# Attention with a spectral mix on one core: a new hand-written order for the last loop, two pairs summed half by VectorE and half by GpSimd, and one pair's x taken earlier

## The chip, the cores and the metric

The kernel runs on one core of a Trainium2 chip. The metric is the device time of one execution in microseconds (us), as the median over several executions. Engines are named as in the profile: PE (TensorE matmul), PEld (its weight loads), DVE (VectorE), ACT (ScalarE), POOL (GpSimd), SP (the engine that issues most of the transfers on and from the chip at the end).

## What is computed

Eight batches, 8 heads, 576 tokens, 64 values a head. First a causal attention with a bias from a running sum of `s`, then a mixing layer over the 512 joined values:

```
attn = softmax(scale * q k^T + min(bias, 0), causal) ; x = attn v      # (8, 576, 512)
X = rfft(x, axis=1);  Y[:, :64] = X[:, :64] * (w_r + i w_i)            # one 512x512 matrix for each of 64 modes
y = irfft(Y, n=576);  u = x + y
out = u + relu(u @ w_ch)
```

The two mode weights have 64 x 512 x 512 values each in float32; reading them is the largest transfer of the program.

## The kernel before

**Stages.** Attention runs over 32 steps `n` (a pair of heads and a batch each), and the products of the modes, which need the weights as they arrive, are spread over these steps. GpSimd issues all weight loads (line 234), SP the small transfers and the output. After the attention comes the last group of modes: `modes(NG - 1, c)` for the chunks c = 0 to 7 of 8 modes each. Each chunk gives `yb` (line 487), its transpose `yt` (672), and for the later chunks `v = y @ w_ch` (680). The results must be regrouped by batch into `yv`: the early chunks by `gather`, which is matmuls into PSUM and copies by ACT and DVE in turn (lines 699, 709, 711), the last two by `spread`, a transfer on SP (line 498). All this shares two PSUM buffers (`auxpool`).

**Pairs.** The output is made in 18 pairs of token tiles, 0 to 17; pairs 1 and 15 are made of the short last tiles of four batches. Each needs z = (x + y) @ w_ch and u = x + y. The product x @ w_ch needs no y, so for the pairs 2 to 17 (`kept`) it is computed early and stored in SBUF (`keep`, or `first_product` for pairs 3 to 8 within the attention). For the pairs 0 and 1 it is left in PSUM: `x_transposed` (transposes, line 635, and DVE casts, 639) and then `x_times_wch` (648). The function `work` takes the kept pairs between the chunks.

**Ways.** How a stored product meets the rest is a letter for each pair:
- "g": ACT copies z (which is y @ w_ch) from PSUM (`relu`, line 795), GpSimd adds the stored product (`gpsimd_sum`, 803), DVE does max and sum in one instruction (`finish`, 819).
- "v": DVE adds z and the stored product (`kept_sum`, 812), then 819.
- "s": ACT writes the stored product into PSUM ahead of the matmuls (`seed`, 894), they add to it, ACT does the Relu (797), DVE adds u (821).
- "e": the product is stored as two half-precision numbers (526, 527), which PE adds by matmuls with the identity (`digits`, 899), then as "s".

**The last loop.** Its order is one string of steps, each a letter and a pair, with a or b for the half: X (x into the bank of u, 774), U (y into it, 744), Z (y @ w_ch, 744), S, E, K, R, G for the helpers above, and F, which sums and starts the output transfer. Each engine takes its instructions in the order of that string. Z has four PSUM banks, by parity of the pair and half, so a Z waits until the last pair of its parity has been read there. U has two double banks by parity, so X of a pair waits for F of the pair two before. The pairs in `x_pool` get their x from GpSimd (line 807) and not from X. Ahead of the loop, `first_u` and `first_z` start the pairs 0 and 1 between the products of the last chunk (the `meanwhile` of `modes`).

Of the kernel before, what the change touches and what calls it, by code (L numbers as in the profile page):

```python
# [18 lines left out]
def kernel(  # L19
# [20 lines left out]
    NG = DM // P  # L40
# [6 lines left out]
    NCK = NM // MC  # L47
# [155 lines left out]
    def ring_of(k):  # L203
        if k < NE:
            return None
        return int(k < LW2 and (k - NE) % (WA + WB) >= WA)
# [38 lines left out]
    for n in range(N):  # L245
# [3 lines left out]
        while nt < min(w, len(wq)):  # L249
            i = ring_of(nt)  # L250
# [245 lines left out]
    def spread(c, which, rows):  # L496

        nc.sync.dma_start(out=yv[16 * c : 16 * c + 16, :, which, :], in_=rows)
# [8 lines left out]
    kept = list(range(NPRE, len(pairs)))  # L507


    ways = dict(zip(kept, "gvgesggsgsgsgsgs"))  # L510

    first_pairs = [i for i in kept[1:] if pairs[i][0][1] < NF and pairs[i][0][0] <= 4][:6]
    z1s, xts1 = {}, {}
# [42 lines left out]
    with tc.tile_pool(name="sc_psum", bufs=2, space=PSUM) as scpool, \  # L556
# [7 lines left out]
        for n in range(N):  # L564
# [11 lines left out]
            i = first_pairs[n - N + len(first_pairs)] if n >= N - len(first_pairs) else None  # L576
# [46 lines left out]
    def parts(b, T):  # L623

        if T < NF:
            return [(slice(0, P), b, ident16h)]
        return [(slice(NL * i, NL * i + NL), b + i, ident16h[:NL, :NL]) for i in range(2)]

    def x_transposed(i):
        xts[i] = xt_sb[len(xts) % 2]  # L630
        for x, (b, T) in enumerate(pairs[i]):
            ps = upool.tile([P, DT, P], FP32, name="xt_ps", tag="u")
            for rows, bb, ident in parts(b, T):
                for dt in range(DT):
                    nc.tensor.matmul(
                        ps[:, dt, rows], x_all[: rows.stop - rows.start, dt, bb, T, :],
                        ident, start=True, stop=True, skip_group_check=True,
                    )
            nc.vector.tensor_copy(out=xts[i][:, x], in_=ps)  # L639

    def start_z(i, x):
        zs[i, x] = zpool.tile([P, DM], FP32, name="z_ps", tag=f"z{i % 2}{x}")

    def x_times_wch(i, last):
        for x in range(2):
            start_z(i, x)
            for dt in range(DT):
                nc.tensor.matmul(  # L648
                    zs[i, x], xts[i][:, x, dt, :], wch_sb[:, dt, :],
                    start=(dt == 0), stop=(last and dt == DT - 1), skip_group_check=True,  # L650
                )
# [25 lines left out]
    def y_times_wch(c, yt):  # L677
        vp = auxpool.tile([P, DM], FP32, name="v_ps", tag="aux")
        for dt in range(DT):
            nc.tensor.matmul(  # L680
                vp, yt[:, dt, :], wch_sb[:, dt, :], start=(dt == 0), stop=(dt == DT - 1)
            )
        vb = spool.tile([P, DM], FP16, name="v_sb", tag="v")
        nc.vector.tensor_copy(out=vb, in_=vp)
        spread(c, 1, vb)
        return vb

    def gather(c0, c1, turns, kinds):

        n = 2 * MC * (c1 - c0)  # L690
        rows = slice(2 * MC * c0, 2 * MC * c1)
        ng = P // n
        for b0 in range(0, B, ng):
            for which in kinds:
                ps = auxpool.tile([P, DM], FP32, name="g_ps", tag="aux")
                for dt in range(DT):
                    for g in range(ng):
                        op = yt_first[:, dt, : c1 - c0].rearrange("p c (x b) -> p (c x) b", b=B)
                        nc.tensor.matmul(  # L699
                            ps[n * g : n * g + n, :] if which else ps[n * g : n * g + n, bass.ts(dt, P)],  # L700
                            op[:, :, b0 + g],
                            wch_sb[:, dt, :] if which else ident16h,
                            start=(dt == 0 or not which), stop=(dt == DT - 1 or not which),
                            tile_position=(0, n * g), skip_group_check=True,
                        )
                for g in range(ng):
                    dst, src = yv[rows, b0 + g, which, :], ps[n * g : n * g + n, :]
                    if g % 2:
                        nc.vector.tensor_copy(out=dst, in_=src)
                    else:  # L710
                        nc.scalar.copy(out=dst, in_=src)
            if b0 // ng in turns:
                work()
# [4 lines left out]
    def work():  # L718

        if not order_z and not ahead:  # L720
            return
        if order_z:
            i = order_z.pop(0)
            x_transposed(i)
            ahead.append(i)
        if len(ahead) == 2 or not order_z:
            i = ahead.pop(0)
            keep(i)
# [3 lines left out]
    TAKE = (3, 2, 4, 0, 0, 0)  # L732
    us, rs = {}, {}
    last = len(pairs) - 1
    x_pool = (17,)
    direct = (2,)
    GK = P - 2 * MC * NX

# [41 lines left out]
    def u_of(i):  # L780
        return [us[i][:, x, :] for x in range(2)]
# [8 lines left out]
    def relu(i, x):  # L790

        if i not in rs:
            rs[i] = result(i)
        if ways.get(i) == "g":
            nc.scalar.copy(out=rs[i][:, x], in_=zs[i, x])
        else:
            nc.scalar.activation(out=rs[i][:, x], in_=zs[i, x], func=ACTF.Relu)

    def gpsimd_sum(i, x):

        r = rs[i][:, x]
        if ways.get(i) == "g":
            nc.gpsimd.tensor_tensor(out=r, in0=r, in1=z1s[i][:, x], op=ALU.add)
        else:
            b, T = pairs[i][x]
            r = r.rearrange("p (g d) -> p g d", d=P)
            nc.gpsimd.tensor_tensor(out=r, in0=r, in1=x_all[:, :, b, T, :], op=ALU.add)
# [6 lines left out]
    def finish(i, x=None):  # L814
        xx = slice(0, 2) if x is None else slice(x, x + 1)
        b, T = pairs[i][0]
        o, u = rs[i][:, xx, :], us[i][:, xx, :]
        if ways.get(i) in ("v", "g"):
            nc.vector.scalar_tensor_tensor(out=o, in0=o, scalar=0.0, in1=u, op0=ALU.max, op1=ALU.add)
        else:  # L820
            nc.vector.tensor_tensor(out=o, in0=u, in1=o, op=ALU.add)
        if T == NF:
            j = b // 2
            dst = out.rearrange("(j h) t e -> j (h t) e", h=2)[j : j + 2, NF * P : NF * P + P, :]
            nc.sync.dma_start(out=dst.rearrange("x p e -> p x e"), in_=o)
        else:
            dst = out[b, bass.ds(first_token(b, T + (x or 0)), P * (2 if x is None else 1)), :]
            nc.sync.dma_start(out=dst.rearrange("(x p) e -> p x e", p=P), in_=o)
# [4 lines left out]
    for c in range(NCK - 2):  # L833
        yb = modes(NG - 1, c)
        for x in range(TAKE[c] - 1):
            work()
        if c == NCK - 3:
            x_transposed(0)
        yt = y_transposed(yb, c)
        if TAKE[c]:  # L840
            work()
        if c >= NY:
            if c == NCK - 3:
                x_times_wch(0, False)
            y_times_wch(c, yt)
            if c == NCK - 3:
                gather(NY, NCK - 2, (), (0,))
        elif c == NY - 1:
            gather(0, NY, (1, 3), (1, 0))
    assert not order_z and not ahead  # L850
    c = NCK - 2
    yb6 = modes(NG - 1, c)
    x_transposed(1)
    yt = y_transposed(yb6)
    x_times_wch(1, False)
    vb6 = y_times_wch(c, yt)


    def first_u():
        add_x(0)  # L860
        add_y(u_of(0), 0, 0, slice(0, GK))
        add_last(u_of(0), 0, yb6, c=0)

    def first_z(i):
        add_y(z_of(i), i, 1, slice(0, GK))
        add_last(z_of(i), i, vb6, c=0)

    yb = modes(NG - 1, NCK - 1, {2: lambda: (first_u(), first_z(0)), 3: lambda: first_z(1)})

    yt = spool.tile([P, DT, P], FP16, name="yt_sb", tag="yt")  # L870
    for x in range(2):
# [49 lines left out]
        "F": finish,  # L921
    }
    for step in (
# [7 lines left out]
    ).split():  # L931
        i = int(step[1:].rstrip("ab"))
        if step[-1] in "ab":
            steps[step[0]](i, "ab".index(step[-1]))
        else:
            steps[step[0]](i)
# [30 lines left out]
```

The softmax here doesn't subtract the row's maximum and nothing guards it: scores larger than these inputs give would overflow.

## Time and profile before

| what | us |
|---|---|
| median of four executions | 444.44 |
| lowest, highest | 443.68, 445.47 |
| the profiled execution, its own time | 443.68 |
| its span, first to last instruction | 441.6 |
| busy over the span: PE, DVE, ACT, POOL | 343.8, 253.0, 226.4, 246.4 |
| output, 18 pairs of 512 KB: first and last transfer issued | 412.65, 438.0 |
| mean of one: line 803 POOL, 819 DVE, 821 DVE (a whole pair) | 1.28, 1.22, 1.22 |
| mean of one: line 795 ACT, 797 ACT, 894 ACT | 0.62, 0.63, 0.63 |

Times are counted from the start of the span. A group of instructions is shown with its busy time, the mean of one in ns, and the idle time of its engine just ahead of it with what ended that. Matmuls overlap, so their mean is longer than the step from one to the next. "Landing" is the time from the issue of a transfer to its end.

### The profile page before, as it was taken

What the parts mean: (1) busy time and instruction counts of PE and PEld (TensorE: products, weight loads), DVE (VectorE), ACT (ScalarE), POOL (GpSimd) and SP (SyncE); (2) the same over time, 40 slices, a digit from 0 to 9 for tenths busy, and PEclk for the clock granted to TensorE, in tenths of its full rate; (3) what the DMA queues carried; (4) which work ended last, traced back from release to release, by engine and by line L of the source; (5) the groups of instructions that cost most, each with busy time, mean ns of one, the idle gap of its engine ahead of it and who ended that gap; (6) DMA issues with size and microseconds to landing.
All of it is one profiled execution on the core that took longest, in us unless ns stands there. A gap on an engine that the chain in (4) does not pass through costs nothing.

```text
span 441.6 us, 10830 instructions
## 1 busy us (share of the span) xinstructions
PE 343.8 (78%) x4411; PEld 207.2 (47%) x4411; DVE 253.0 (57%) x574; ACT 226.4 (51%) x421; POOL 246.4 (56%) x385
## 2 busy tenths in 40 slices
PE   1688988998776996793946927988996887779994
PEld 1465665555554653462534504555553435434441
DVE  7766775675645664462633605667656443452696
ACT  1576785465644643472543514565661524420794
POOL 7766565565565656455655546555544444440495
PEclk9998998998969798898895968999999989988998
DMA  9999999999999999999999999999999999998498
GB/s 178 202 207 205 204 207 205 207 201 205 209 200 208 204 208 204 208 207 208 204 206 206 208 207 192 210 205 208 204 209 211 209 209 209 210 216 167 149 388 343
DMA packets 72768, 93.25 MB, mean 211 GB/s; under 512 B 29760, under 2 KB 31296, under 8 KB 72720
## 3 DMA queue, kind: packets, MB, share of 16 engines
q0 software_dynamic: 63408, 81.29, 105.0%
q1 hardware_dynamic: 9312, 11.29, 7.6%
q8 instruction: 34, 0.56, 0.5%
q14 instruction: 14, 0.11, 0.1%
HBM read 163.51 MB, written 9.44 MB: 392 GB/s over the span
## 4 chain that ended last, share of the span: by engine, by line
DMA 53%; PE 25%; DVE 11%; issue 4%; POOL 3%; ACT 3%; POOLq 0%; SPq 0%; DVEq 0%; ACTq 0%
DMA w_sb<-in_moe_w_i_dram 27%; DMA w_sb<-in_moe_w_r_dram 17%; DMA qk<-in_k_dram 4%; PE z_ps L648 4%; PE yp L463 4%; DMA qk<-in_q_dram 4%; PE sc_ps L382 3%; DVE qt L344 2%; PE av_ps L418 2%; PE sc_ps L376 2%; PE tr_ps L340 2%; POOL w_sb L234 2%; PE g_ps L699 1%; DVE kt L344 1%; DVE xs L453 1%
## 5 line engine op out<-in xcount | busy, mean ns | idle before, releaser
L390 ACT ACTIVATE p_sb<-sc_ps,cumt_sb 128x576 f16<-128x576 f32 (+1 forms) x256 | 141.8, 636 | 34.2 <-PE sc_ps L382 33.8
L234 POOL DMA_DIRECT2D w_sb<-in_moe_w_r_dram x120 | 71.2, 595 | 61.2 <-DMA w_sb<-in_moe_w_i_dram 16.7
L234 POOL DMA_DIRECT2D w_sb<-in_moe_w_i_dram x120 | 70.9, 593 | 51.4 <-DMA w_sb<-in_moe_w_i_dram 18.6
L382 PE MATMUL sc_ps<-qt,kt 128*128 128x512 bf16 (+2 forms) x384 | 78.1, 316 | 3.9 <-ACT kt L344 3.3
L344 DVE COPY qt<-tr_ps 64x576 bf16<-64x576 bf16 x64 | 47.8, 747 | 56.8 <-PE tr_ps L340 56.8
L234 POOL DMA_DIRECT2D v<-in_v_dram x72 | 52.1, 724 | 38.3 <-DMA w_sb<-in_moe_w_r_dram 10.2
L340 PE MATMUL tr_ps<-ident,qk 64*64 64x64 bf16 x1152 | 35.5, 206 | 39.7 <-DMA qk<-in_k_dram 17.6
L463 PE MATMUL yp<-w_sb,xs 128*32 128x512 bf16 (+1 forms) x480 | 43.9, 418 | 22.0 <-DMA w_sb<-in_moe_w_i_dram 14.8
L361 ACT ACTIVATE p<-sc_ps,cumt 128x64 f16<-128x64 f32 x32 | 10.1, 314 | 89.9 <-PE sc_ps L357 89.9
L376 PE MATMUL sc_ps<-negm,ident 128*128 128x256 bf16 x256 | 54.2, 297 | 0.0
L382 PEld LDWEIGHTS <-kt 128*128 128x128 bf16 x384 | 39.2, 106 | 31.5 <-ACT kt L344 8.7
L340 PEld LDWEIGHTS <-qk 64*64 64x64 bf16 x1152 | 27.0, 119 | 55.7 <-DMA qk<-in_k_dram 18.5
L418 PE MATMUL av_ps<-v,p_sb 128*128 128x65 f16 x1024 | 43.5, 196 | 1.5 <-DVE x_all L428 0.6
L418 PEld LDWEIGHTS <-p_sb 128*128 128x128 f16 x1024 | 37.0, 99 | 8.8 <-DVE x_all L428 4.2
L453 DVE CAST xs<-ft_ps 64x128 bf16<-64x128 f32 x128 | 36.6, 286 | 3.3 <-PE ft_ps L443 1.7
L463 PEld LDWEIGHTS <-xs 128*32 128x32 bf16 (+1 forms) x512 | 19.2, 145 | 40.4 <-DMA w_sb<-in_moe_w_i_dram 15.2
L423 DVE TENSOR_REDUCE den<-av_ps 128x5 f32<-128x10 f32 x64 | 10.8, 169 | 41.4 <-PE av_ps L418 40.4
L428 DVE TENSOR_TENSOR x_all<-av_ps,rcp 128x320 f16<-128x320 f32 x64 | 31.5, 491 | 2.2
L344 ACT COPY kt<-tr_ps 64x576 bf16<-64x576 bf16 x32 | 22.9, 715 | 14.7 <-DVE qt L344 14.1
L648 PE MATMUL z_ps<-wch_sb,xs 128*128 128x512 f16 x96 | 25.6, 415 | 0.2 <-DVE xs L639 0.2
L443 PE MATMUL ft_ps<-Ff_sb,x_all 128*64 128x192 f16 (+1 forms) x320 | 24.6, 268 | 1.0 <-DVE x_all L428 1.0
L483 DVE TENSOR_TENSOR y_acc<-yp,y_acc 128x512 f32<-128x512 f32 x16 | 11.1, 692 | 24.3 <-PE yp L463 23.5
(113 smaller groups left out, 435.3 us busy)
## 6 DMA issues: line engine op xcount, KB each, us to landing
w_sb<-in_moe_w_r_dram POOLq DMA_DIRECT2D x120, 256.0 KB, 8.5
w_sb<-in_moe_w_i_dram POOLq DMA_DIRECT2D x117, 256.0 KB, 9.0
out_dram<-r_w SPq DMA_DIRECT2D x16, 512.0 KB, 2.8
v<-in_v_dram POOLq DMA_DIRECT2D x72, 64.0 KB, 7.5
qk<-in_q_dram POOLq DMA_DIRECT2D x15, 288.0 KB, 8.4
qk<-in_k_dram POOLq DMA_DIRECT2D x15, 288.0 KB, 9.2
x_all<-in_moe_w_i_dram POOLq DMA_DIRECT2D x6, 256.0 KB, 7.7
y_acc<-in_moe_w_r_dram POOLq DMA_DIRECT2D x4, 256.0 KB, 7.8
```

The source lines that it names most:

```text
L234: nc.gpsimd.dma_start(out=dst, in_=src)
L340: nc.tensor.transpose(ps[rows, r, :], src[rows, r, :], ident16[rows, rows])
L344: copy(out=to[:, :, :, half * RH : half * RH + RH], in_=ps[HP * i : HP * i + HP].rearrange("d r (h p) -> d h p r", h=2),)
L376: nc.tensor.matmul(ps[:, bass.ds(w * S, W)], ident16, negm[:, bass.ts(r, W)], start=True, stop=False, skip_group_check=True,)
L382: nc.tensor.matmul(ps[:, c0 : c0 + i1 - i0], keys[:, w, r, :], qh[:, i0:i1], start=False, stop=True, skip_group_check=True,)
L390: nc.scalar.activation(out=pt[:, poff[x] : poff[x] + S - w * W], in_=ps[:, w * S : (w + 1) * S - w * W], func=ACTF.Exp, bias=cumt_sb[:, x, ...
L418: nc.tensor.matmul(ps[:, I, r : r + NCH], lhsT, rhs, start=(i == 0), stop=(i == len(todo) - 1), skip_group_check=True,)
L428: nc.vector.tensor_tensor(out=x_all[:, g, b, :, D * h : D * h + D], in0=ps[:, :, 1 : NCH], in1=rcp.unsqueeze(2).to_broadcast([P, NT, D]), ...
L443: nc.tensor.matmul(ps[HP * q_ : HP * q_ + HP].rearrange("p h f -> p (h f)"), x_all[:nT, g, b, T, q_::2], Ff_sb[:nT, T, :], start=(T == 0), ...
L453: nc.vector.tensor_copy(out=xs[g % 2][HP * h : HP * h + HP, q_, :, h, :, b, :], in_=a)
L463: nc.tensor.matmul(ps[32 * cg : 32 * cg + 32, :], cols[k0:, q_, 1 - ri, :, c * MC // 2 + cg], wt[(g, c, ri, cg // 2)][k0:, 2 * (cg % 2) + ...
L648: nc.tensor.matmul(zs[i, x], xts[i][:, x, dt, :], wch_sb[:, dt, :], start=(dt == 0), stop=(last and dt == DT - 1), skip_group_check=True,)
```

## The change

Pair by pair, 2 to 17, the ways go from `gvgesggsgsgsgsgs` to `vsgmsgsgmsgsgsgs`. A new letter "m" is treated by `relu`, `gpsimd_sum` and `finish` as "g" is; in the string, half a of such a pair (5 and 10) is a K on DVE and half b an R and a G. No pair is "e" any more. (The letter "n" is accepted and not used.) Pair 17 gets its x from PE. The order string of the last loop is another one. Ahead of the loop, the transposes of pair 1 stand before `y_times_wch` of chunk 5 and its products behind the second gather, and both `first_z` come ahead of `first_u`.

```
-    ways = dict(zip(kept, "gvgesggsgsgsgsgs"))
+    ways = dict(zip(kept, "vsgmsgsgmsgsgsgs"))
...
-    x_pool = (17,)
+    x_pool = ()
...
-        if ways.get(i) == "g":
+        if ways.get(i) in ("g", "m", "n"):
...
-        if ways.get(i) in ("v", "g"):
+        if ways.get(i) in ("v", "g", "m", "n"):
...
             if c == NCK - 3:
                 x_times_wch(0, False)
+                x_transposed(1)
             y_times_wch(c, yt)
             if c == NCK - 3:
                 gather(NY, NCK - 2, (), (0,))
+                x_times_wch(1, False)
...
     yb6 = modes(NG - 1, c)
-    x_transposed(1)
     yt = y_transposed(yb6)
-    x_times_wch(1, False)
     vb6 = y_times_wch(c, yt)
...
-    yb = modes(NG - 1, NCK - 1, {2: lambda: (first_u(), first_z(0)), 3: lambda: first_z(1)})
+    yb = modes(NG - 1, NCK - 1, {2: lambda: (first_z(0), first_z(1)), 3: first_u})
...
-        "R0a X1 R0b F0a U1 R1a F0b Z2a R1b Z2b R2a F1 X2 R2b G2a U2 Z4a Z4b R4a Z3a Z3b G2b K3a X3 R4b U3 "
-        "S6a K3b E5a S6b G4a F2 Z5a E5b R5a Z5b Z6a R5b Z7a G4b F3 Z6b X4 R6a Z7b R6b U4 R7a Z8a F4 Z8b X5 "
-        "R7b G7a U5 S9a S9b X6 F5 G7b U6 R8a Z9a R8b Z9b F6 X7 R9a G8a U7 R9b Z10a F7 Z10b S11a X8 G8b "
-        "S11b U8 R10a Z11a X9 R10b G10a U9 F8 R11a Z12a Z12b R12a Z11b F9 G10b X10 R12b U10 S13a Z14a R11b "
-        "Z14b G12a F10 Z13a R14a X11 U11 S13b Z16a G12b R13a F11 X12 R14b U12 S15a Z13b G14a Z16b F12 X13 "
-        "R13b U13 R16a Z15a G14b S15b F13 X14 R15a U14 R16b Z15b G16a F14 X15 S17a R15b U15 G16b S17b Z17a "
-        "F15 X16 R17a U16 Z17b G17a F16 U17 R17b G17b F17a F17b "
+        "R0a X1 R0b F0a U1 R1a F0b Z2a R1b Z2b S3a K2a X2 S3b F1 U2 Z3a Z3b R3a Z4a K2b X3 R4a U3 F2 R3b "
+        "G4a Z5a S6a Z4b Z5b R4b K5a Z6a X4 R5b G4b F3 U4 S6b Z7a Z7b R6a Z6b G5b F4 R7a X5 U5 R6b Z9a R7b "
+        "G7a F5 X6 S8a Z9b U6 S8b Z8a G7b R9a F6 X7 U7 R8a Z8b R9b G9a Z10a F7 X8 R8b U8 S11a Z10b K10a "
+        "G9b X9 S11b U9 F8 R10b Z12a Z11a G10b R12a Z12b Z11b F9 R12b X10 U10 R11a G12a Z14a R11b F10 Z14b "
+        "X11 S13a U11 G12b S13b Z13a F11 X12 R14a U12 R13a G14a Z16a Z13b R14b F12 X13 R13b U13 G14b S15a "
+        "Z16b F13 X14 S15b U14 R16a Z15a F14 Z15b R16b G16a X15 R15a U15 R15b G16b S17a X16 F15 S17b U16 "
+        "Z17a Z17b R17a F16 X17 R17b U17 F17a F17b "
```

More of the change, by code (lines that the diff above doesn't have):

```diff
@@ L801, in gpsimd_sum @@
         r = rs[i][:, x]
-        if ways.get(i) == "g":
+        if ways.get(i) in ("g", "m", "n"):
             nc.gpsimd.tensor_tensor(out=r, in0=r, in1=z1s[i][:, x], op=ALU.add)
```

## The prediction, made before the changed kernel ran

> **What bounds the kernel now.** I read the page's 40 slices first, then windows of 4 us over the end, the groups of the last loop by shape, the chain of its last 10 us, the output transfers by issue time, and last the granted clock on a fixed grid.
>
> ```profile
> span 441.6 us, 10830 instructions
> ...
> 412.00:416.00 4.00, 4.00 (x24) 1.62 (x20) 3.11 (x5) 3.53 (x8) 1.94 (x2) 1.00 0.56 206
> ...
> 420.00:424.00 4.00, 3.93 (x19) 1.65 (x17) 3.89 (x4) 4.00 (x9) 4.00 (x4) 1.00 0.95 370
> ...
> 432.00:436.00 4.00, 3.80 (x20) 1.08 (x18) 3.70 (x4) 3.51 (x7) 3.73 (x4) 1.00 1.05 408
> 436.00:440.00 4.00, 0.00 (x0) 0.00 (x0) 1.62 (x3) 0.00 (x0) 1.29 (x2) 0.85 1.03 400
> ```
>
> The columns are window, PE, PEld, DVE, ACT, POOL, clock, DMA share, GB/s. Until 405 the weights fill the DMA engines. From 411.3 the last loop runs, and from 420 everything in it is full: PE, ACT, POOL, nearly DVE, and from 428 the output DMA too.
>
> ```profile
> L803 POOL TENSOR_TENSOR r_w<-r_w,z 128x512 f32<-128x512 f32 x12 | 14.9, 1277 | 0.8 <-ACT r_w L795 0.8
> L819 DVE SCALAR_TENSOR_TENSOR r_w<-r_w,u_ps 128x1024 f32<-128x1024 f32 x9 | 10.9, 1219 | 1.3 <-POOL r_w L803 1.2
> L797 ACT ACTIVATE r_w<-z_ps 128x512 f32<-128x512 f32 x16 | 9.5, 628 | 0.5 <-PE z_ps L744 0.3
> ...
> 434.35 0.60 ACT r_w L797
> 434.95 0.07 issue
> 435.02 1.15 POOL r_w L807
> 436.17 1.12 POOLq L962
> 437.30 0.02 issue
> 437.32 0.69 DVE r_w L821
> ```
>
> The idle columns are almost empty. The chain ends in pair 17: two GpSimd additions of x in series between the last Relus and the last sums. POOLq L962 is the second of them.
>
> ```profile
> L234 POOL DMA_DIRECT2D w_sb<-in_moe_w_i_dram x1: 590/590/590, 396.6 to 396.6; - x1
> DMA to landing us min/median/max: 10.5/10.5/10.5
> ...
> 407.15 0.19 PEld L463 LDWEIGHTS <-xs 128*32 128x32 bf16 x4 [0.42 <-DMA w_sb<-in_moe_w_i_dram]
> ```
>
> The last weights land at 396.6 + 10.5 = 407.1, and the products that need them start at 407.15. So what stands ahead of the loop is tied between PE and the weights.
>
> **The change, part by part.**
>
> *x of pair 1 moved.* Its transposes (16 matmuls, 0.96 in the chain) go ahead of y_times_wch of chunk 5, its 8 matmuls (2.98) behind the second gather. Before, both stood after chunk 6's modes. With them move two DVE casts (1.28 for both), now ahead of chunk 5's v_sb. Second v_sb and gather slip by about 0.65. PE idled 392.98 to 394.86 while yv was copied, and the 8 matmuls (1.83 at full clock, as the same group took at 380.7) fit there. Chunk 6's modes then start near 395.45 instead of 394.86, but their second half waits for weights until 396.35 either way. Behind it PE is freed of about 3.9. SP's order stays: the spread of chunk 6's v only goes out about 3 us sooner (near 400.4 instead of 403.53), with no output transfer to pass. POOL's weight issues keep their order, at a constant landing of 10 to 10.6. **Sum: 0**, because the weights still land at 407.1. Without that cover it would be up to 3.9 of gain. Swapping first_u and first_z reorders 1.40 against 0.98 ahead of the same last product: 0.
>
> *Ways.* By number of instructions in the loop, with the step from one start to the next read from runs of the same instruction:
> - POOL: 18 to 14. Four of about 1.25 go, two of them at the very end (2.27).
> - ACT: 46 both times. Copies 16 to 14 (12 for "g", 2 for "m"), Relus 18 both times, seeds 12 to 14: 22.4 to 22.5 at 0.46, 0.49 and 0.52.
> - DVE: K from 2 to 4 at 0.62, plus 16 double sums at 1.14 and 4 single ones at 0.62: 22.0 to 23.2.
> - PE: four digit matmuls go, two of X17 come, at 0.216: −0.43 of about 23.
>
> Pair 5's two L527 subtractions (0.69 each) leave DVE near 302, in the weight-bound part: 0. POOL stops being a bound; DVE takes its place.
>
> *New waits.* Z7a stands behind K5a, Z12a behind K10a, F2 behind K2b. PE has X, U and Z of other pairs queued behind each. F1 now waits at DVE behind K2a, so its transfer leaves at 415.25 instead of 414.65.
>
> *New order.* I wrote the new order out as queues by hand, from R0a at 411.30, each instruction starting when its engine has stepped on and its operand is there (0.04 to pass; 0.38 from a matmul's start to its result). Landmarks of the new one: S3a 413.24, R3a 414.89, F1 issued 415.25, K2b 415.13, F2 417.0, R4b 416.84, F3 418.75, G4b to 418.74, F4 420.0, G5b to 419.97, F5 421.25, then F8 425.5, F10 427.8, F13 431.5, F15 434.2, F16 435.4. X17 starts at 434.25 after F15 has freed its banks, U17 ends at 435.27, F17a and F17b follow back to back; F17b is issued at 436.6. The trace has 420.74 for F4, 436.36 for F16 and 438.04 for F17b. **Engines: −1.4.**
>
> *The output queue.* 512 KB land 2.7 to 2.8 after the issue if nothing is ahead, and 2.9 to 3.1 if the last one is recent. Landings of before run 423.4 (F4) to 440.54 (F17b): 13 pairs in 17.14, of which about 0.6 with the engines below full share (0.69 at 421, 0.89 at 426). So one pair needs about 1.28. After: F3 lands 421.55, F4 at 422.83, F7 at 426.67; F8 is late (425.5 + 2.8 = 428.3); from there 9.0 pairs of 1.28 give 439.82. **Output: 439.82 − 440.54 = −0.7.** Half of the engines' gain is lost in the queue.
>
> *The rule on bandwidth.* The windows show 400 to 408 GB/s with the engines full. The Trainium skill, "DMA: Bandwidth & Descriptors", "Where 436 GB/s comes from", puts the ceiling at 435 GB/s. At 435 a pair takes 1.205, the queue drains, and the gain would be the engines' −1.4. The row decides: 1.28.
>
> *The rule on the clock, which speaks for calm.* "TensorE: Matmul & The Clock Gate", "Part 1: The HAM clock gate", says that the clock halves after an idle window of about 3.4 us and returns after a busy one. PE's longest new gap is under 2 us, so by the rule nothing happens. The trace is stricter:
>
> ```profile
> 32.64:36.05 3.41, 1.85 (x43) 1.00 1.25 204
> ...
> 367.14:370.56 3.42, 1.92 (x24) 1.00 1.12 209
> ...
> 391.04:394.45 3.41, 1.56 (x36) 1.00 1.12 224
> 394.45:397.86 3.41, 3.00 (x26) 0.50 1.12 221
> 397.86:401.28 3.42, 3.42 (x20) 0.50 1.13 211
> ```
>
> Columns: window, PE busy, clock, DMA. On one grid of 3.413, a window with 1.85 busy or less is followed by half clock, one with 1.92 is not; 3.00 did not bring it back, 3.42 did. In the new order 391.04 to 394.45 has about 3.0 (safe, where before it halved), but 397.86 to 401.28 only 1.76, as PE now waits for weights landing at 401.7. So half clock from 401.3 is likely by the trace, not by the rule. From 401.7 to the end of the last products PE has 4.73 of work (0.30, z 0.86 and 0.98, 0.58, u 1.40, 0.61), due at 407.82: 1.39 of slack, which hides 2.8 us of half clock. One window of 3.4 costs 0.3 at most, two up to 2.0. I take 0 and keep 0 to 2.0.
>
> Sum: 441.6 − 0.7 = 440.9 of span, with the 2.08 outside it 443.0 against this execution's 443.68. That execution is the fastest of the four; I move the median: 444.44 − 0.7 = **443.7**.
>
> **Rivals.**
> 1. *The front gains or the queue gives way.* If transfers sustain the 412 to 414 GB/s of single windows, or if other executions of before lost time to half clock ahead of 407 (PE and weights were tied there, so any later return of the clock delays the loop), the gain is −1.4 to −2: 443.0 to 442.4. For: the profiled execution is 0.76 under the median. Against: 400 to 408 over each long window.
> 2. *Half clock ahead of the loop, slower.* Two windows at half clock, ending at e: the delay is (e − 401.7)/2 − 1.39, so 0.96 for 406.4 and 1.8 for 408.1. Less 0.7 this ends 0.3 to 1.1 slower, typically 445.3; with the loop's gain lost also, 446. It decides from a delay of 0.7, that is once half clock lasts beyond 405.9. For: 1.76 is below 1.85. Against: the same page calls the windows free-running, which one trace cannot show; other positions of the grid give 1.9 to 2.0 and no halving.
> 3. *The order does nothing.* DVE at 23.2 with K in between delays the sums by what POOL gave back: 444.4.
>
> **How the numbers follow.** The forecast has 0.50, rival 1 0.22, rival 2 0.20, rival 3 0.08. 0.3% is 1.33 us, about what a measurement of this kernel can tell from no change. Faster than 443.11 takes most of rival 1 and a little of the forecast: 0.22. Slower than 445.77 takes over half of rival 2: 0.14. Within: 0.64. The range, 442.4 to 445.8, reaches over rival 1 and most of rival 2; the forecast's own is 443.1 to 444.3.
>
> **What would show it.** Right: no L807 and no L899, F17b issued 1 to 1.5 earlier against R0a, output share at 1.03 or more from F4 on, landings of 3 us or more near the end, the last L463 still at 407.1. Half clock between 401 and 408 with R0a past 412.5 shows rival 2; landings staying at 2.8 with the last issue 1.4 earlier, rival 1. I am wrong if R0a moves ahead by over 0.5, or if F8 to F16 take longer than before's 10.26.

## The result and the profile after

The changed kernel takes 443.85 us at the median of 40 executions, the kernel before 444.46 of 63 beside it: a ratio of 0.9988, 95% interval 0.9983 to 0.9994. That is 0.6 us faster, inside the 0.3% that was set as no change; 443.7 had been forecast.

The profiled execution has a span of 442.0 and a time of 444.08, so it is no faster than the profiled one of before (441.6 and 443.68), which was 0.8 under its kernel's median. The windows of 4 us (columns as before: PE, PEld, DVE, ACT, POOL, clock, DMA share, GB/s) and the instruction that starts the end of the front:

```profile
span 442.0 us, 10817 instructions
...
412.00:416.00 4.00, 4.00 (x25) 1.41 (x23) 3.02 (x4) 3.27 (x7) 0.00 (x0) 1.00 0.46 164
...
420.00:424.00 4.00, 4.00 (x19) 1.75 (x18) 3.84 (x4) 4.00 (x9) 4.00 (x4) 1.00 0.94 363
424.00:428.00 4.00, 4.00 (x20) 1.74 (x18) 3.96 (x5) 3.78 (x9) 4.00 (x4) 1.00 0.98 380
...
432.00:436.00 4.00, 4.00 (x23) 1.31 (x22) 3.55 (x4) 3.86 (x9) 2.71 (x3) 1.00 1.05 408
436.00:440.00 4.00, 0.41 (x2) 0.00 (x0) 1.75 (x3) 0.30 (x1) 0.00 (x0) 1.00 1.05 408
...
408.04 0.65 PE L463 MATMUL yp<-w_sb,xs 128*32 128x512 bf16 x4 [0.31 <-DMA w_sb<-in_moe_w_i_dram]
```

POOL is no longer full at the end, and the output still leaves at 408 GB/s. DVE is fuller from 424 to 428, where before it had this:

```profile
424.00:428.00 4.00, 4.00 (x19) 1.74 (x18) 3.37 (x4) 4.00 (x9) 3.98 (x4) 1.00 1.01 390
```

The last products stand at 408.04 in place of 407.15: in this execution the last weights landed 0.9 later, and PE waited for them. That alone moves everything behind it. So I read the loop from its own start, the first Relu (R0a), before and after:

```profile
411.30 1.09 ACT L797 ACTIVATE r_sb<-z_ps 128x512 f32<-128x512 f32 x2 [1.94 <-PE z_ps L755]
...
412.18 1.08 ACT L797 ACTIVATE r_sb<-z_ps 128x512 f32<-128x512 f32 x2 [1.95 <-PE z_ps L755]
```

The groups of the loop by shape, and the end of the chain of waits:

```profile
L803 POOL TENSOR_TENSOR r_w<-r_w,z 128x512 f32<-128x512 f32 x10 | 12.5, 1280 | 19.2 <-ACT r_w L795 19.2
L819 DVE SCALAR_TENSOR_TENSOR r_w<-r_w,u_ps 128x1024 f32<-128x1024 f32 x9 | 10.9, 1215 | 0.2
L797 ACT ACTIVATE r_w<-z_ps 128x512 f32<-128x512 f32 x16 | 9.7, 638 | 0.7 <-PE z_ps L744 0.5
...
435.98 0.45 PE u_ps L744 x2
436.43 0.03 DVEq L821
436.46 0.00 DVE r_w L819
436.46 0.04 issue
436.51 0.69 DVE r_w L821
437.20 0.60 DVEq L962
```

The 19.2 of idle at POOL is the time before its first addition. DVE's idle time ahead of L819, 1.3 before with 1.2 of it for POOL, is 0.2. The chain now ends in PE and the two single sums (DVEq L962 is the second); the two GpSimd additions of x are gone.

The last output transfers, kernel before first, then after (issue, then time to landing: F17b before; F14, then F17a and F17b after):

```profile
L828 SPq DMA_DIRECT2D out_dram<-r_w x1: 344/344/344, 438.0 to 438.0; - x1
DMA to landing us min/median/max: 2.5/2.5/2.5
```

```profile
L828 SPq DMA_DIRECT2D out_dram<-r_w x1: 372/372/372, 433.7 to 433.7; - x1
DMA to landing us min/median/max: 3.4/3.4/3.4
...
L828 SPq DMA_DIRECT2D out_dram<-r_w x2: 344/373/402, 437.2 to 437.8; - x2
DMA to landing us min/median/max: 3.0/3.0/3.0
```

From R0a, F17b is issued after 26.7 before and 25.6 after: the engines gained 1.1. The last landing is after 29.2 and 28.7: the output gained 0.5. The other 0.6 is in the longer landing. The table has the same two distances for every kernel that ran, free of when the weights landed. They are read to 0.01 us from the one profiled execution of each, and then rounded:

| kernel | R0a | F17b issued, from R0a | last landing, from R0a | ratio to before, interval |
|---|---|---|---|---|
| before | 411.3 | 26.7 | 29.2 | |
| after | 412.2 | 25.6 | 28.7 | 0.9988 (0.9983 to 0.9994) |
| front_only | 412.1 | 26.7 | 29.2 | 1.0004 (0.9996 to 1.0012) |
| loop_only | 412.0 | 25.6 | 28.7 | 0.9986 (0.9978 to 0.9994) |
| tail_pe | 412.3 | 26.3 | 29.2 | 1.0014 (1.0004 to 1.0023) |
| before_half | 411.5 | 26.7 | 28.4 | 0.9990 (0.9980 to 1.0000) |
| after_half | 412.7 | 25.6 | 27.3 | 0.9957 (0.9940 to 0.9974) |
| after_4k | 412.6 | 25.6 | 28.5 | 0.9978 (0.9970 to 0.9985) |
| after_warm | 411.8 | 25.6 | 30.0 | 1.0026 (1.0017 to 1.0035) |
| after_warm2 | 411.7 | 25.6 | 28.7 | 0.9991 (0.9982 to 1.0000) |
| after_pad | 412.6 | 25.6 | 29.9 | 1.0024 (1.0016 to 1.0031) |
| after_rows | 411.9 | 26.3 | 30.3 | 1.0018 (1.0011 to 1.0025) |
| after_rows3 | 412.6 | 25.6 | 28.4 | 0.9982 (0.9975 to 0.9989) |

### The profile page after: what moved, and what is told of

Same layout as the page of the kernel before. It is cut to its first block, busy times and chain, and to the rows that moved or that the text cites. A ratio compares the mean times of both kernels' runs of the same rounds, so it can differ in the third digit from the quotient of the medians.

```text
span 442.0 us, 10817 instructions
## 1 busy us (share of the span) xinstructions
PE 343.4 (78%) x4409; PEld 206.2 (47%) x4409; DVE 252.7 (57%) x574; ACT 226.0 (51%) x421; POOL 241.5 (55%) x381
## 4 chain that ended last, share of the span: by engine, by line
DMA 63%; PE 18%; DVE 9%; issue 4%; POOL 4%; ACT 1%; SPq 0%; DVEq 0%; POOLq 0%; ACTq 0%
DMA w_sb<-in_moe_w_i_dram 37%; DMA w_sb<-in_moe_w_r_dram 15%; DMA qk<-in_k_dram 11%; PE sc_ps L382 3%; POOL w_sb L234 2%; PE yp L463 2%; DVE qt L344 2%; PE tr_ps L340 2%; PE sc_ps L376 2%; PE u_ps L774 2%; DVE xs L453 2%; PE u_ps L744 2%; PE z_ps L744 1%; DVE x_all L428 1%; PE av_ps L418 1%
## 5 line engine op out<-in xcount | busy, mean ns | idle before, releaser
L463 PE MATMUL yp<-w_sb,xs 128*32 128x512 bf16 (+1 forms) x480 | 44.0, 414 | 21.3 <-DMA w_sb<-in_moe_w_i_dram 16.4
L463 PEld LDWEIGHTS <-xs 128*32 128x32 bf16 (+1 forms) x512 | 19.4, 144 | 40.9 <-DMA w_sb<-in_moe_w_i_dram 16.5
L524 ACT COPY z<-z_ps 128x512 f32<-128x512 f32 x22 | 12.9, 586 | 23.5 <-PE z_ps L546 14.1
L344 DVE COPY kt<-tr_ps 64x576 bf16<-64x576 bf16 x32 | 24.4, 763 | 0.4
(108 smaller groups left out, 429.2 us busy)
```

Of the source, the lines that this page charges most:

```text
L344: copy(out=to[:, :, :, half * RH : half * RH + RH], in_=ps[HP * i : HP * i + HP].rearrange("d r (h p) -> d h p r", h=2),)
L463: nc.tensor.matmul(ps[32 * cg : 32 * cg + 32, :], cols[k0:, q_, 1 - ri, :, c * MC // 2 + cg], wt[(g, c, ri, cg // 2)][k0:, 2 * (cg % 2) + ...
```

## The experiments

My theory: the weights set the start of the loop, and behind them the output transfers, 1.28 us a pair, take back about half of what the engines gain. The rivals are that the front (the part ahead of the loop) brings the gain, that half clock ahead of the loop costs time, and that the chain of the last instructions sets the end.

### The two parts alone: front_only and loop_only

```
front_only: before, with
+                x_transposed(1)                    (ahead of y_times_wch of chunk 5)
+                x_times_wch(1, False)              (behind the second gather)
-    x_transposed(1)
-    x_times_wch(1, False)
-    {2: lambda: (first_u(), first_z(0)), 3: lambda: first_z(1)}
+    {2: lambda: (first_z(0), first_z(1)), 3: first_u}
loop_only: after, with these lines as before
```

> The kernel before with only the part ahead of the loop changed: transposes of pair 1 ahead of chunk 5's product, its matmuls behind the second gather, both first_z ahead of first_u. Theory (the weights set the start of the loop): no change, 444.5 within 0.2, the last L463 starts with the landing of the last weights. Rival (half clock ahead of the loop delays R0a): 0.5 to 1.8 us slower, with the last L463 well behind the last landing. Rival (PE was late in many executions of before): 0.4 to 0.8 us faster, which would then be the whole gain.

Measured 444.51 beside 444.36.

> The changed kernel with the part ahead of the loop as before: only ways, x_pool and the order string differ from before. Theory: the gain is all here, 0.6 us faster than before (443.85). Rival (the front brings the gain): 444.4.

Measured 443.89, 0.5 faster. So the gain is in the loop, and none is shown for the front. The timeline of front_only shows why:

```profile
407.97 0.65 PE L463 MATMUL yp<-w_sb,xs 128*32 128x512 bf16 x4 [0.80 <-DMA w_sb<-in_moe_w_i_dram]
```

PE stood idle for 0.80 for the last weights. What the move takes from PE ends in this wait.

### The end alone: tail_pe

```
-    x_pool = (17,)
+    x_pool = ()
-        "... X16 R17a U16 Z17b G17a F16 U17 R17b G17b F17a F17b "
+        "... X16 R17a U16 Z17b F16 X17 U17 R17b F17a F17b "
```

> The kernel before with only pair 17's x taken from GpSimd to PE: X17 behind F16 in the order, G17a and G17b gone; the ways and the rest of the order as before. Theory (the output transfers queue at 1.28 us a pair): F17b is issued about 1.1 earlier, but the last landing stays within 0.2 of F16's landing plus 1.28, so 0 to 0.2 us faster. Rival (the chain of the last instructions sets the end, as the chain of waits has it): 1.1 us faster, 443.3.

Measured 444.71, 0.1% slower than before. My own figure for the engines was wrong here: F17b is issued only 0.4 earlier (26.3 for 26.7 from R0a), because F16 ends no sooner and F17a and F17b are each 0.6 of DVE behind it. The last landing is at 29.2, as before, so even the 0.4 is lost in the queue. The rival with 1.1 falls: removing the additions that end the chain of waits gains nothing.

The slower median does not come from inside the span, whose median is 442.3 for tail_pe and for the kernel before beside it. Six of the 22 executions spent 3.15 to 3.9 us outside the span; the other 16, and all of the kernel before, spent 2.0 to 2.1. The profiled execution is one of the six (446.03, with a span of 442.6). Between 444 and 446, behind its last instruction, it has one more packet in the instruction queue q8 (packets, MB, share of the window):

```profile
q8 instruction: 1, 0.02, 4.3%
```

It is this kernel's 35th, where before has 34. That this packet takes the time, in this execution and in the other five, is not shown.

### The output halved: before_half and after_half

```
-            nc.sync.dma_start(out=dst.rearrange("(x p) e -> p x e", p=P), in_=o)
+            dst = dst.rearrange("(x p) e -> p x e", p=P)
+            if x is None:
+                nc.sync.dma_start(out=dst[:, :1], in_=o[:, :1])
+            else:
+                nc.sync.dma_start(out=dst[:, :, : DM // 2], in_=o[:, :, : DM // 2])
...
(and the first of the two tiles only for the short pairs)
```

> The kernel before, writing only half of the output: of each pair only the first tile (256 KB in the same 2 KB pieces), of the single halves of pairs 0 and 17 the first 256 columns. All the engines' instructions stay. Theory (output queues at 1.28 us a pair): the queue is gone, landings 2.0 to 2.3 us throughout, the end follows F17b's issue: about 0.5 us faster than before (444.0). Rival (output is not a bound): at most 0.3 us faster.

> The changed kernel, writing only half of the output in the same way. Theory (output queues): the engines' whole gain shows, F17b issued 1.1 to 1.4 us earlier after R0a than in the kernel before with half the output, so 1.1 to 1.4 us between these two, about 442.8. Rival (the engines gain only 0.6): the two differ by 0.6 as the full kernels do.

Measured 443.89 and 442.15, where the medians of the full kernels differ by 0.6. From R0a the last landing is 28.4 and 27.3, a difference of 1.1, exactly that of the issues. The medians differ by 1.7; after_half has only six executions, four near 442.1 and two near 443.2, and why this is more than 1.1 stays open. The issue of F13 in after_half, and of F16 and F17a:

```profile
L830 SPq DMA_DIRECT2D out_dram<-r_w x1: 333/333/333, 433.1 to 433.1; - x1
DMA to landing us min/median/max: 2.0/2.0/2.0
...
L830 SPq DMA_DIRECT2D out_dram<-r_w x1: 333/333/333, 437.0 to 437.0; - x1
L832 SPq DMA_DIRECT2D out_dram<-r_w x1: 332/332/332, 437.8 to 437.8; - x1
DMA to landing us min/median/max: 1.7/1.9/2.0
```

Every landing is 2.0 at most, so there is no queue, and the engines' gain arrives whole. This is what shows that the output took the other 0.6.

### Half clock ahead of the loop: after_warm, after_warm2 and after_pad

In the changed kernel the clock did halve, as the trace of before had suggested, but for one window of the grid (window, PE busy, clock, DMA share, GB/s):

```profile
395.79:399.20 3.41, 1.05 (x10) 1.00 1.13 222
399.20:402.61 3.41, 2.91 (x10) 0.51 1.12 210
402.61:406.03 3.42, 2.77 (x20) 0.99 0.91 189
```

after_warm fills PE's waits there:

```
+    def filler(n):
+        ps = upool.tile([P, DM], FP32, name="fill_ps", tag="u")
+        for _ in range(n):
+            nc.tensor.matmul(ps, ident16h, wch_sb[:, 0, :], start=True, stop=True, skip_group_check=True)
...
-    yb6 = modes(NG - 1, c)
+    yb6 = modes(NG - 1, c, fill=7)
+    filler(2)
     yt = y_transposed(yb6)
+    filler(2)
     vb6 = y_times_wch(c, yt)
+    filler(4)
...
(filler(3) behind both first_z)
```

> The changed kernel with 18 extra matmuls (identity by the mixing matrix, into a free PSUM bank, read by nobody) in PE's waits between chunk 6's modes and the last products, so that the clock is not halved there. Theory (half clock there is hidden by the wait for weights): clock 1.0 from 395 to 408, the time as the changed kernel's, 443.85 within 0.2. Rival (half clock costs in part of the executions): 0.3 to 0.8 us faster than the changed kernel.

Measured 445.23, 1.4 slower than the changed kernel, which neither theory nor rival had said. R0a was no later, and F17b was issued at 25.6 from it as in the changed kernel, but from the transfer issued at 432.2 on the landings went from 3.1 to 4.6. The list of DMA queues had 35 instruction packets in place of 34. So I made the filling without more instructions:

```
after_warm2: after_warm with 7, 2, 2, 3 and 2 fillers, and in product()
+            if g == 1 and c in (2, 3, 4, 5) and ri == 0 and q_ == 1:
+                return
```

> As after_warm, with 16 extra matmuls, and 16 of the mode products left out much earlier (one product group of four chunks of the second weight group), so that PE has as many instructions as the changed kernel. after_warm had one instruction packet more (35 for 34 in the queue of instructions) and landings of 4.6 us from the output issued at 432.2 on, 1.4 us slower. Theory (that packet took the time): 34 packets, landings of 3.0 to 3.4, the time as the changed kernel's, 443.85 within 0.2. Rival (the extra matmuls themselves cost): 445.2 again. Rival (half clock ahead of the loop costs): 443.1 to 443.5.

Measured 443.68, with the clock at 1.0 from 394 to 410 and 34 packets. The changed kernel has 443.85, and the two intervals overlap: the fillers cost nothing that shows, and full clock there gains nothing that the medians can tell.

Half clock is not free in every execution, though. In the profiled one of after_4k (below), which has the changed kernel's front, it lasted two windows, 400.02 to 406.84. Behind them stand the issue and landing of the last weights, and the last products:

```profile
400.02:403.43 3.41, 2.88 (x11) 0.50 1.12 223
403.43:406.84 3.41, 3.41 (x15) 0.50 0.66 131
...
L234 POOL DMA_DIRECT2D w_sb<-in_moe_w_i_dram x1: 592/592/592, 396.3 to 396.3; - x1
DMA to landing us min/median/max: 11.0/11.0/11.0
...
408.46 0.65 PE L463 MATMUL yp<-w_sb,xs 128*32 128x512 bf16 x4
```

The weights landed at 407.3, and PE started on them only 1.2 later, without an idle gap: here PE was late, and R0a with it. The same distance is 0.5 in the profiled execution of after_pad (half clock from 399.09 to 405.92) and 0.8 in that of tail_pe (395.43 to 402.25, with the front of before). In the other ten it is 0.05 at most.

after_pad has the instructions only:

```
+            if n == 20:
+                ps = auxpool.tile([P, DM], FP32, name="fill_ps", tag="aux")
+                for _ in range(18):
+                    nc.tensor.matmul(ps[:, :P], ident16h, ident16h, start=True, stop=True, skip_group_check=True)
```

> The changed kernel with 18 extra matmuls (128 columns each, read by nobody) in the attention's step 20, 36 instructions as in after_warm but nowhere near the end. Theory (a 35th instruction packet falls into the output): 35 packets, landings of 4 us and more in the last output transfers, about 1.4 us slower than the changed kernel, 445.2. Rival (after_warm was slow through work near the loop): 443.85 within 0.2.

Measured 445.38. Its list of queues over the whole span and in the window from 434 to 435, and the transfers issued at 432.9 and at 436.8 and 437.6:

```profile
q8 instruction: 35, 0.57, 0.5%
...
q8 instruction: 1, 0.02, 5.5%
...
L832 SPq DMA_DIRECT2D out_dram<-r_w x1: 372/372/372, 432.9 to 432.9; - x1
DMA to landing us min/median/max: 4.5/4.5/4.5
...
L832 SPq DMA_DIRECT2D out_dram<-r_w x2: 344/358/372, 436.8 to 437.6; - x2
DMA to landing us min/median/max: 4.2/4.3/4.3
```

18 matmuls at 199.5, over two hundred microseconds ahead of the loop, delay the output's end by 1.2. The packet stands where the landings jump: between 434 and 435 here and between 433 and 434 in after_warm, in the full output. In the changed kernel the last one before the end of the output comes between 411 and 412, ahead of the first output transfer. What the DMA engines moved from 440 to 444, in slices of 0.1 us, in the changed kernel and in after_pad:

```profile
GB/s 410 348 226 21 0 0 0 0 0 0 0 0 0 0 0 0 0 0 0 0 0 0 0 0 82 0 0 0 0 0 0 0 0 0 0 0 0 0 0 0
...
GB/s 410 430 430 369 410 369 144 21 41 20 20 20 41 20 21 20 41 20 20 20 21 0 0 0 0 0 0 0 0 0 0 0 0 0 0 0 0 0 0 0
```

In after_pad the full rate ends at 440.6, and some 26 GB/s go on to 442.1. That is a sixteenth of 410, so most likely one DMA engine of the sixteen finishes alone. That it is the one that brought the packet is inferred: the packet itself takes 0.9 (5.5% of 16 engines' 1 us), less than the 1.2 to 1.4 by which the landings are late.

### Larger pieces: after_4k, after_rows and after_rows3

```
after_4k:
-            nc.sync.dma_start(out=dst.rearrange("(x p) e -> p x e", p=P), in_=o)
+            nc.sync.dma_start(out=dst.rearrange("(p x) e -> p x e", p=P), in_=o)
```

> The changed kernel with each partition's two rows of a pair written next to each other (4 KB pieces in place of two of 2 KB; the rows land in another order than the output's, the amount is the same). Theory: if larger pieces move faster than 408 GB/s, the output queue shortens by up to 0.7 us, 443.1 to 443.6; if the rate is the engines' of the DMA whatever the piece, 443.85 within 0.2. Rival (output is not a bound): 443.85 whatever the rate shows.

Measured 443.47, 0.4 faster than the changed kernel by the medians, though the intervals of the two still touch. Its landings from F2 on are 2.6 to 3.1, where the changed kernel has 2.7 to 3.4, and its output runs at 420 GB/s from 428 to 432, where the changed kernel has 407. So the rate does depend on the piece, and the time points the same way. The next two write the same pieces in the output's order.

```
after_rows:
+    tok = np.arange(NF * P).reshape(NF // 2, P, 2).transpose(0, 2, 1).reshape(-1)
+    Ff_np[: NF * P] = Ff_np[tok]
+    G_np[:, : NF * P] = G_np[:, tok]
...
+                    o = poff[x] + I // 2 * W + I % 2 - w * W
+                    cols = pt[:, o : o + 2 * P - 1 : 2]
...
+            for h in range(2):
+                dst = out[b + h : b + h + 3 : 2, NF * P :, :]
+                nc.sync.dma_start(out=dst.rearrange("x p e -> p x e"), in_=o[NL * h : NL * h + NL])
...
+            dst = out[b, bass.ds(T * P, 2 * P), :].rearrange("(p x) e -> p x e", p=P)
```

> The changed kernel with neighbouring tokens on one partition: the two tiles of a pair hold the even and the odd tokens of 256, so that each partition writes 4 KB pieces as in after_4k, now in the output's order. For that the attention's second product takes every second column of p (stride 4 bytes in the weight loads), the constants are permuted, all batches start at token 0, and each of the two pairs of short tiles is written by two transfers of 256 KB. Theory: landings of 2.6 us where nothing is ahead and about 0.4 us faster than the changed kernel, 443.4 to 443.5, as after_4k. Rival (the strided weight loads slow PE): L418's loads well above 99 ns; hidden behind the weights unless PE falls behind them. Rival (two short transfers on 64 partitions): up to 0.5 us lost in pair 15, 443.9.

Measured 445.25. The strided weight loads cost nothing (99 ns as before), but each transfer on 64 partitions is slow: 3.2 us for 256 KB with nothing ahead of it, where F0a has 2.0 for as much on 128. They hold up what follows, at both pairs of short tiles:

```profile
436.00:440.00 4.00, 0.18 (x1) 0.00 (x0) 1.52 (x3) 0.06 (x1) 0.00 (x0) 1.00 0.91 279
440.00:444.00 4.00, 0.00 (x0) 0.00 (x0) 0.00 (x0) 0.00 (x0) 0.00 (x0) 0.67 0.33 129
```

after_rows3 keeps the short tiles as they were and pays with small matmuls in the attention's second product:

```
+                    p0 = max(0, (w * W - t0) // 2)
+                    o = poff[x] + t0 + 2 * p0 + I % 2 - w * W
+                    todo.append((p0, I, r, pt[:, o : o + 2 * (P - p0) - 1 : 2], vv, (0, p0) if p0 else None))
...
+            for x in range(2):
+                todo.append((P - NL // 2, NF - 2 + x, 1, p4[n % 2][rows, x:NL:2], v4[g % 2][rows, b, :NCH], (NL * h, P - NL // 2)))
...
+            dst = out[b, bass.ds(first_token(b, T), 2 * P), :].rearrange("(p x) e -> p x e", p=P)
+            nc.sync.dma_start(out=dst[:, xx], in_=o)
```

> As after_rows, but with the odd batches still starting at token 64, so that a pair of short tiles is written by one transfer on 128 partitions, as in the changed kernel. Price: 96 small matmuls more in the attention (192 PE instructions). Theory (after_rows lost its gain in the short tiles' two transfers on 64 partitions, with landings of 3.2 to 4.5): landings of 2.6 to 3.1, 0.4 us faster than the changed kernel, 443.4 to 443.5. Rival (the longer instruction stream moves a packet into the full stretch of the output): landings above 4 and 1 us or more slower. Rival (4 KB pieces in the output's order bring nothing): 443.85.

Measured 443.67, 0.9982 of before (0.9975 to 0.9989). The output runs at 419 GB/s:

```profile
428.00:432.00 4.00, 4.00 (x20) 1.78 (x19) 3.84 (x4) 4.00 (x10) 3.95 (x4) 1.00 1.02 419
432.00:436.00 4.00, 4.00 (x23) 1.27 (x22) 3.54 (x4) 3.87 (x9) 3.13 (x3) 1.00 1.03 419
```

It is the lowest of the kernels that compute everything, clear of before, but its interval overlaps that of the changed kernel, so a gain over that one is not shown. Of the 0.4 of after_4k, the traces have 0.2 to 0.3 (28.5 and 28.4 against 28.7 from R0a). It has 35 packets too, without a jump in its landings (3.1 at most): its last one before the end of the output comes between 416 and 417, when the output is not yet full.

## Why the prediction was right

*The front at 0.* Right for the median, as front_only shows, with PE idle for the last weights. The sign "the last L463 still at 407.1" was too strict: the last weights landed between 407.1 and 408.5 in the 13 profiled executions.

*The engines at −1.4.* The mechanism was right, the size a little high: 1.1. The hand-made queue follows the trace closely. Shifted by 0.9 for R0a, F4 was forecast at 420.9 and issued at 421.0, F8 426.4 and 426.5, F13 432.4 and 432.6, F16 436.3 and 436.5, F17b 437.5 and 437.8. The missing 0.3 appears at F15 (435.1 forecast, 435.4 issued), where DVE waited 0.45 for ACT's Relu. Of the 1.1, tail_pe has 0.4 from GpSimd leaving the end alone; the other 0.7 comes only with the new ways and the new order.

*The output queue at 1.28 a pair.* Right, though the sum it came from, (17.14 − 0.6)/13, gives 1.27. From F8's landing to the end, 429.2 to 440.9, nine pairs took 11.7, or 1.30 each. The halved output shows that this, and no engine, took the difference between 1.1 and 0.5; 0.7 had been forecast for the output. One sign failed: the output's share was 0.94 and 0.98 up to 428, and 1.05 only from there. The Trainium skill's 435 GB/s ("DMA: Bandwidth & Descriptors", "Where 436 GB/s comes from") would have left room that 2 KB pieces did not have, with 407 to 408; 4 KB pieces came to 420. The same section takes about 358 as what binds transfers between HBM and SBUF, which the output here exceeds.

*The clock.* The halving came after a window with 1.05 of 3.41 busy, against the wording of an idle window in the Trainium skill ("TensorE: Matmul & The Clock Gate", "Part 1: The HAM clock gate"). In this execution it cost nothing, as the central value said: PE had the wait for weights to hide it in. That the median shows no cost either is in part luck of where the windows fall. After_4k's execution has the two windows of rival 2, ending at e = 406.84, and rival 2's own formula, (406.84 − 401.7)/2 − 1.39, gives 1.2, as measured there. The limits of 1.85 and 1.92 read from one trace do not hold in the others. The clock stayed full after a window with 1.53 busy in loop_only, and halved after one with 2.28 in the changed kernel (window, PE busy, clock, DMA share, GB/s, first loop_only):

```profile
353.57:356.98 3.41, 1.53 (x17) 1.00 1.13 211
356.98:360.40 3.42, 3.42 (x23) 1.00 1.12 208
...
334.41:337.82 3.41, 2.28 (x23) 1.00 1.12 210
337.82:341.24 3.42, 2.95 (x20) 0.50 1.11 212
```

Another reading failed too: 3.00 of 3.41 had been taken as too little for the clock to return, and in the changed kernel it returned after 2.91.

*The rivals.* The front's gain is refuted by front_only, and an order that does nothing by loop_only. Half clock as the usual case is refuted by the median and by after_warm2, but single executions show its delay. The part of rival 1 in which the queue gives way did not happen with the pieces as they are.

## What to carry to other kernels

When several engines and the output are all near full, a gain on the engines is paid out only as far as the slowest stream behind them allows: compare the issue of the last transfer with its landing, from a common start, and halve the output once to see how much the queue keeps. A chain that ends in one engine's instructions does not promise their time: here taking two of them out gained nothing. And an experiment that adds instructions can cost time far from where it adds them, so keep their number the same and look at where in time the instruction packets fall. A median without a cost also does not show that every execution is without it: here PE was late behind half clock in three profiled executions of thirteen.

## What was not expected of the hardware

- 36 PE instructions more brought a 35th instruction packet (0.57 MB in place of 0.56) into the full output, at 433 to 435, and with it 1.2 to 1.4 us on every output landing from there on, in two kernels with the instructions in quite different places. 192 more also had 35 packets, but the last one before the end of the output at 416 to 417, and no such jump. That the packet causes it fits all three and their places in time; how it costs more than its own 0.9 stays open.
- Output in 4 KB pieces moved at 419 to 420 GB/s from 428 to 432, in 2 KB pieces (the changed kernel) at 407.
- 256 KB on 64 partitions landed after 3.2 us, on 128 partitions after 2.0.
